# One chain of row statistics under transposes of the identity, own PSUM banks for the first projection, held spills, and earlier third gate weights

## The chip, the cores and the metric

The kernel runs on one core of one Trainium2 chip. The metric is the device time of one execution in microseconds (us). Three runs of the kernel before gave 2610.35, 2610.72 and 2611.09 us, so the median is 2610.72 us.

## What is computed

One block of attention with 32 heads, and beside it a gated feed-forward block on the same normalised rows. The silu of the feed-forward result gates the attention result.

```python
def _A_ref(x, wqkv, wo):                      # H = 32 heads of Dh = 18
    qkv = (x @ wqkv).reshape(B, S, 3, H, Dh).transpose(2, 0, 3, 1, 4)
    q, k, v = qkv[0], qkv[1], qkv[2]
    p = softmax(einsum("bhqd,bhkd->bhqk", q, k) * Dh ** -0.5)
    o = einsum("bhqk,bhkd->bhqd", p, v)
    return o.transpose(0, 2, 1, 3).reshape(B, S, D) @ wo

def _B_ref(x, W_gate, W_up, W_down):          # F = 4608
    gate, up = x @ W_gate, x @ W_up
    return (relu(gate) * up) @ W_down

xn = layernorm(x)                             # x: [1, 2048, 576] fp32
out = x + _A_ref(xn, wqkv, wo) * silu(_B_ref(xn, W_gate, W_up, W_down))
```

## The kernel before

All products are in fp32, made of pairs of fp32r numbers: each operand is split into a high part (a cast) and a low part (what the cast left over), and a product is the sum of hi x hi, hi x lo and lo x hi. So each weight and each activation costs a cast (on ScalarE or GpSimd) and a subtraction (on VectorE or GpSimd) before TensorE can use it. Weights are split on GpSimd by `split_pool` (lines 130 to 134).

The kernel has three stages. In the first (lines 302 to 644) the 2048 rows are taken in four groups g of 512. Of each group the rows are normalised, turned by TensorE into features x rows ("tps" banks), split, and kept as five tiles x of [128, 2, 512]. Then come the projections: four blocks b of q and k (`qk_block`, one `job` each, weights wqk0 to wqk3), the last 64 columns for two groups together (`qk_last`, wqk4), and four jobs of v (`v_job`, one for each 128 rows). A `job` (lines 469 to 479) issues 30 matmuls of its first part into two PSUM banks, then a tiny ScalarE instruction "mark" that waits for them, then the 24 matmuls of the second part of the job before (`flush`). The two halves of a job run side by side on the two halves of the array's rows. q, k and v go to DRAM (qd, kd, vd) by DMAs that GpSimd issues. `spill(g)` (lines 438 to 441) writes the five x tiles of a group to DRAM (xTd), four DMAs of 128 x 1024 fp32 (512 KB) and one of 64 x 1024. They are read back as nine tiles of 64 features by `load_x` (lines 293 to 300), two DMAs of 256 KB each, for the second stage.

The second stage takes the feed-forward block in 144 units (g, f): `up(k)` makes gate and up for 128 columns of F (27 matmuls on each half), `up_end` the product hh = relu(gate) x up and its split, and `down(k)`, after every second unit, adds two units' products into four y tiles. The gate and up weights of unit k are loaded by `load_up` into one of two buffers rg and split by `split_up` into one of two buffers gw. Between the matmuls of the units stand the attention matmuls: scores for the row maxima ("pm", 512 keys at a time), scores for the exponential ("psx") and the product with v ("po"). The row maxima of the first head pair begin already in the v jobs of the last group (`max_steps`, dealt one step per 18 matmul pairs). They read q and k of this pair from strips: q in the tile kq, the keys in four chunks c of 512 positions, chunk 0 in kA and chunks 1 to 3 in kq (`load_q`, `load_k`; six DMAs of 18 rows each). The third stage is the output projection.

What sets the order. The operations on TensorE, GpSimd and (up to unit 10) the DMAs issued by SyncE are kept in program order; each engine works its list from the front, and an instruction that waits holds up all behind it. SyncE issues all the loads, the spills and the strips; of the eight semaphores that its DMAs use in turn, each DMA waits until the one eight places ahead of it has landed. `load_x` in the second stage is not pinned after unit 10, so a scheduler may place it earlier.

Places that the change and the prediction speak of: `first_rows` (lines 387 to 420) normalises group 0, with two chains of statistics for rows 0, 1 and 2, 3 of its four row blocks, and splits wqk0 on ScalarE and VectorE; GpSimd's split of wqk1 waits for that (line 558). `next_pair` (line 445) hands out PSUM banks: "shared" is a pool of five, "bank" one of two, psO a single one. v weights are loaded in lines 564 to 568 and called at lines 603 to 607. `spill(g)` is called at line 638, the six loads `load_x(0, c)` behind it for g = 2 at line 641, `spill(3)` at line 575, and the gate weights of units 0 and 1 at lines 594 and 599. In `emit_unit` (line 863) the third weights, of unit 2, are loaded with unit 0 (line 869) and split with unit 1 (line 868).

## Time and profile before

| | us |
|---|---|
| median of three runs | 2610.72 |
| the profiled execution | 2611.43 |
| its span, first to last instruction | 2609.7 |
| granted TensorE clock, mean | 1.000 |
| VectorE busy | 1900.1 |
| ScalarE busy | 1383.3 |
| GpSimd busy | 1197.8 |

All times are of this one execution, in us from the start of its span. Rows of the timeline give start, duration, engine, source line, operation, tiles (out<-in), how many instructions are merged into the row, and in brackets the idle time of the engine before it with what ended it. PE is a matmul, PEld the weight load beside it, DVE is VectorE, ACT ScalarE, POOL GpSimd, SPq a DMA issued by SyncE. A row of the timeline whose engine is SPq shows the issuing alone; the data lands later. Rows of the windows give a stretch, its length, busy time and number of instructions for PE, PEld, DVE, ACT and POOL, the granted clock, the mean busy share of the 16 DMA engines, and GB/s.

### The profile page before, as it was taken

Reading aid. Unit: us, or ns where it says so; the run is one execution under the profiler, and the core shown is the slowest. Engines: PE = TensorE matmul, PEld = TensorE weight load, DVE = VectorE, ACT = ScalarE, POOL = GpSimd, SP = SyncE. Lnnn points to the kernel's source line nnn. Section 1 sums busy time; section 2 is a strip of 40 time slices with the busy share of each in tenths; the row PEclk is TensorE's granted clock in tenths of the full one; section 3 lists DMA queues with packets and bytes.
Section 4 is the critical chain, followed back from the end, with each engine's and each line's share of the span. In section 5 each row is a group of like instructions: output and inputs, shape, how many; then the busy total and the mean of one; then the engine's idle time right before and its main releaser. Section 6 shows DMA issues by size and latency. Waiting matters only on the chain.

```text
span 2609.7 us, 54494 instructions
## 1 busy us (share of the span) xinstructions
PE 2590.9 (99%) x21788; PEld 2035.6 (78%) x21788; DVE 1900.1 (73%) x3145; ACT 1383.3 (53%) x2594; POOL 1197.8 (46%) x971
## 2 busy tenths in 40 slices
PE   8999999999999999999999999999999999999999
PEld 7898887777777777777777777777777777777778
DVE  5335678788878788787887787887777878778235
ACT  2321135556665556555666555555556655555642
POOL 5246764344464434443455444444346444434554
PEclk9999999999999999999999999999999999999999
DMA  7867422222542322232363222222253232222245
GB/s 246 274 211 162 104 74 69 70 73 74 116 121 57 82 65 70 58 79 64 80 150 88 67 69 72 65 73 68 71 128 105 73 75 60 76 58 62 67 121 183
DMA packets 263806, 253.11 MB, mean 97 GB/s; under 512 B 27648, under 2 KB 208896, under 8 KB 263552
## 3 DMA queue, kind: packets, MB, share of 16 engines
q1 hardware_dynamic: 255808, 222.48, 32.9%
q0 software_dynamic: 7744, 27.14, 3.1%
q8 instruction: 172, 2.82, 0.5%
q14 instruction: 82, 0.67, 0.1%
HBM read 203.01 MB, written 46.01 MB: 95 GB/s over the span
## 4 chain that ended last, share of the span: by engine, by line
PE 97%; DMA 1%; POOL 1%; DVE 1%; issue 0%; ACT 0%; SPq 0%; POOLq 0%; DVEq 0%; ACTq 0%
PE pg L68 32%; PE po L68 19%; PE py L68 18%; PE pm L68 11%; PE psx L68 9%; PE pq L68 4%; PE pv L68 2%; PE pw L68 2%; DMA rg<-in_B_W_up_dram 0%; PE tps L76 0%; POOL wv L85 0%; DMA xt<-in_A_x_dram 0%; DMA ro<-od 0%; SPq L97 0%; DMA y<-gd 0%
## 5 line engine op out<-in xcount | busy, mean ns | idle before, releaser
L272 DVE TENSOR_REDUCE mx<-pm 128x1 f32<-128x512 f32 x2048 | 1363.9, 689 | 268.8 <-PE pm L68 148.9
L97 ACT ACTIVATE p<-psx 128x512 f32<-128x512 f32 x2048 | 1097.9, 603 | 583.0 <-PE psx L68 541.5
L68 PE MATMUL pg<-x,gw 64*128 64x512 f32 x7560 | 1372.8, 394 | 2.3 <-POOL gw L85 1.8
L68 PEld LDWEIGHTS pg<-x,gw 64*128 64x128 f32 x7560 | 1033.5, 186 | 85.9 <-issue 3.7
L85 POOL TENSOR_TENSOR hh<-h,hh 128x512 fp32r<-128x512 f32 x144 | 184.3, 1280 | 812.7 <-ACT hh L97 790.7
L68 PEld LDWEIGHTS py<-dw,hh 128*128 128x128 f32 x3456 | 460.1, 188 | 56.1 <-issue 31.8
L68 PE MATMUL py<-dw,hh 128*128 128x288 f32 x3456 | 476.8, 297 | 0.0
L68 PE MATMUL po<-p,va 128*32 128x512 f32 x4096 | 465.9, 595 | 0.0
L725 DVE TENSOR_TENSOR y<-py,y 128x288 f32<-128x288 f32 x544 | 244.3, 454 | 225.9 <-PE py L68 225.8
L85 POOL TENSOR_TENSOR gw<-rg,gw 128x1152 fp32r<-128x1152 f32 x144 | 385.9, 2680 | 11.6
L68 PEld LDWEIGHTS po<-p,va 128*32 128x32 f32 x4096 | 119.8, 109 | 276.2 <-issue 265.4
L85 POOL CAST dw<-rd 128x576 fp32r<-128x576 f32 x144 | 95.8, 665 | 387.7 <-PE py L68 382.1
L68 PE MATMUL psx<-qT,kq 56*128 56x512 f32 x608 | 229.8, 392 | 0.0
L68 PE MATMUL pm<-kq,qT 54*128 54x512 f32 x608 | 228.7, 398 | 0.1
L85 POOL TENSOR_TENSOR dw<-rd,dw 128x576 fp32r<-128x576 f32 x144 | 206.3, 1433 | 11.6
L97 ACT ACTIVATE hh<-h 128x512 fp32r<-128x512 f32 x144 | 90.8, 630 | 220.7 <-DVE h L696 220.7
L68 PE MATMUL psx<-kq,kA 56*128 56x512 f32 x512 | 195.4, 393 | 0.3 <-DVE h L696 0.2
L68 PE MATMUL pm<-kq 54*128 54x512 f32 x512 | 195.3, 402 | 0.0
L68 PE MATMUL psx<-kq 56*128 56x512 f32 x512 | 194.2, 392 | 0.0
L68 PE MATMUL pm<-kA,kq 54*128 54x512 f32 x512 | 193.6, 400 | 0.1
L85 POOL CAST gw<-rg 128x1152 fp32r<-128x1152 f32 x144 | 165.4, 1149 | 0.0
L68 PE MATMUL pm<-kA,qT 54*128 54x512 f32 x416 | 159.4, 402 | 0.0
(92 smaller groups left out, 2180.5 us busy)
## 6 DMA issues: line engine op xcount, KB each, us to landing
rg<-in_B_W_gate_dram SPq DMA_DIRECT2D x144, 288.0 KB
rg<-in_B_W_up_dram SPq DMA_DIRECT2D x144, 288.0 KB
rd<-in_B_W_down_dram SPq DMA_DIRECT2D x144, 288.0 KB
x<-xTd SPq DMA_DIRECT2D x72, 256.0 KB
qd<-hh POOLq DMA_DIRECT2D x16, 512.0 KB, 5.0
kd<-hh POOLq DMA_DIRECT2D x16, 512.0 KB, 6.1
xTd<-x SPq DMA_DIRECT2D x16, 512.0 KB
kq<-kd SPq DMA_DIRECT2D x210, 36.0 KB
```

Source lines behind the costliest of these rows:

```text
L68: return tc.keep_in_program_order(nc.tensor.matmul(*args, **kw))
L85: return lambda *args, **kw: tc.keep_in_program_order(op(*args, **kw))
L97: i = op(*args, **kw)
L272: vec(nc.vector.tensor_reduce(mx[:, h, b, j, c : c + 1], ps, axis=AX.X, op=ALU.max))
L725: vec(nc.vector.tensor_tensor(ys[j][:, cs], ps, ys[j][:, cs], ALU.add))
```

## The change

- `first_rows` makes one chain of statistics for all four row blocks. Before it TensorE transposes the identity 57 times into a bank that nothing reads. The cast of wqk0 stands behind the square root; its subtraction is cut in four, two pieces of 256 columns on VectorE and two of 384 and 256 on GpSimd, behind VectorE's.
- The first job takes its banks from the pool of two, not from the shared five.
- The v weights are loaded into three x tiles, early, and split one block earlier (`load_v`); the normalisation of group 1 is dealt every 9 steps and not every 7.
- `spill(g)` of groups 0, 1 and 2 gets a wait: its DMAs stay behind the mark of the group's second v job.
- The loads of x (`load_x`) are pinned to program order.
- The weights of unit 2 are loaded during the v jobs of the last group and split right behind the matmuls of unit 0, ahead of that unit's hh.
- Units 0, 2, ... 14 and 15 take psO and a shared bank, not units 1, 3, ... 15.

```diff
--- before.py
+++ after.py
@@ -127,10 +127,8 @@
         nc.scalar.activation(dhi, ps, AF.Copy)
         nc.vector.tensor_tensor(dlo, ps, dhi.bitcast(F32), ALU.subtract)
 
-    def split_pool(hi, lo, raw, behind=None):
-        cast = gp.tensor_copy(hi, raw)
-        if behind is not None:
-            after(cast, behind)
+    def split_pool(hi, lo, raw):
+        gp.tensor_copy(hi, raw)
         gp.tensor_tensor(lo, raw, hi.bitcast(F32), ALU.subtract)
 
     PRODUCTS = ((0, 0), (0, 1), (1, 0))
@@ -293,9 +291,11 @@
     def load_x(g, c):
         xc = xtile(xA)
         for t in range(2):
-            sp.dma_start(
-                xc[t * R : (t + 1) * R].rearrange("p a s -> p (a s)").bitcast(F32),
-                xTd[g, c // 2, c % 2 * R : c % 2 * R + R],
+            pinned(
+                nc.sync.dma_start(
+                    xc[t * R : (t + 1) * R].rearrange("p a s -> p (a s)").bitcast(F32),
+                    xTd[g, c // 2, c % 2 * R : c % 2 * R + R],
+                )
             )
         xcur.setdefault(g, []).append(xc)
 
@@ -305,7 +305,7 @@
         xB = pool(xBs, "xB", XC, "right")
         hx = pool(xBs, "hx", 4, "right")
 
-        def weights(name, n, parts, pl=one, held=None, behind=None, **kw):
+        def weights(name, n, parts, pl=one, held=None, **kw):
 
             sl = WS if len(parts[0]) == 2 else XC
             gw = homes_w[name] if name in homes_w else pl.tile([P, 2, WS, n], F32R, name=name, **kw)
@@ -318,12 +318,9 @@
                 hi, lo = gw[:, 0, :, o : o + m], gw[:, 1, :, o : o + m]
 
                 if held is not None:
-                    held += [
-                        lambda: pinned(nc.scalar.activation(hi, rg, AF.Copy)),
-                        lambda: vec(nc.vector.tensor_tensor(lo, rg, hi.bitcast(F32), ALU.subtract)),
-                    ]
+                    held += [hi, lo, rg]
                 else:
-                    split_pool(hi, lo, rg, behind)
+                    split_pool(hi, lo, rg)
                 o += m
             return gw
 
@@ -384,40 +381,34 @@
             split_full(xc[:, 0], xc[:, 1], ps)
             xs[g].append(xc)
 
-        def first_rows(xt, split_hi, split_lo):
+        def first_rows(xt, hi, lo, rg):
 
             xn = new_xn()
             banks = [shared("tps") for _ in range(XC)]
-            halves = [(0, 1), (2, 3)]
-            a, b = (stats(xt, js) for js in halves)
-
-            def finish(st_):
+            js = range(4)
+            steps = stats(xt, js)
+            while True:
                 try:
-                    while True:
-                        next(st_)
+                    next(steps)
                 except StopIteration as s:
-                    return s.value
-
-            def norm(js, ln):
-                for _ in normalize(xn, xt, js, *ln):
-                    pass
-
-            for _ in range(3):
-                next(a)
-            next(b)
-            ln = finish(a)
-            for _ in range(2):
-                next(b)
-            norm(halves[0], ln)
-            split_hi()
-            norm(halves[1], finish(b))
-            done = split_lo()
-            for j in range(4):
+                    ln = s.value
+                    break
+            pinned(nc.scalar.activation(hi, rg, AF.Copy))
+            for j, _ in enumerate(normalize(xn, xt, js, *ln)):
                 for c in range(XC):
                     turn(banks[c], xn, j, c)
+            rest = []
+            for s0 in (0, XC):
+                for on, ss in ((nc.vector, slice(s0, s0 + 2)), (None, slice(s0 + 2, min(s0 + XC, WS)))):
+                    args = lo[:, ss], rg[:, ss], hi[:, ss].bitcast(F32), ALU.subtract
+                    if on is None:
+                        rest.append(args)
+                    else:
+                        done = vec(on.tensor_tensor(*args))
+            for args in rest:
+                after(gp.tensor_tensor(*args), done)
             for ps in banks:
                 keep_x(0, ps)
-            return done
 
         def rows_to_features(g, xt):
 
@@ -435,15 +426,19 @@
                     keep_x(g, ps)
                 yield
 
-        def spill(g):
+        def spill(g, behind=None):
             for c in range(XC):
                 m = P if c < XC - 1 else R
-                sp.dma_start(xTd[g, c, :m], xs[g][c][:m].rearrange("p a s -> p (a s)").bitcast(F32))
+                out_ = sp.dma_start(xTd[g, c, :m], xs[g][c][:m].rearrange("p a s -> p (a s)").bitcast(F32))
+                if behind is not None:
+                    after(out_, behind)
 
         njob = [0]
 
         def next_pair(name):
             njob[0] += 1
+            if njob[0] == 1:
+                return [bank(name) for _ in range(2)]
             if njob[0] % 3:
                 return [shared(name) for _ in range(2)]
             return [shared(name), psO.tile([P, 512], F32, tag="po", name=name)]
@@ -466,6 +461,8 @@
                 run(*gens, P2)
                 done()
 
+        marks = []
+
         def job(outs, ops, done):
 
             fence = []
@@ -475,6 +472,7 @@
             for ins in fence:
                 after(seen, ins)
             fence.append(seen)
+            marks.append(seen)
             flush()
             pending.append((gens, done))
 
@@ -554,23 +552,35 @@
 
         held = []
         qk_weights(0, held=held)
-        w0_done = first_rows(rows0, *held)
-        qk_weights(1, behind=w0_done)
+        warm = bank("warm")
+        for _ in range(57):
+            tp(warm[:, :P], ident, ident)
+        first_rows(rows0, *held)
+        qk_weights(1)
         nxt = load_rows(1)
+        wvs = []
+
+        def load_v(m):
+            rg = xtile(xA).bitcast(F32).rearrange("p a s -> p (a s)")[:, : WS * VH]
+            rg = rg.rearrange("p (c f) -> p c f", f=VH)
+            load_nat(rg, [[(wqkv, 2 * D + o * HC + m * VH, VH)] for o in range(2)])
+            wvs.append(rg)
+
+        load_v(0)
         qk_weights(2)
         qk_weights(3)
+        load_v(1)
+        load_v(2)
         wv = one.tile([P, 2, WS, HC], F32R, name="wv")
 
         def v_weights(m):
-            rg = wr.tile([P, WS, P], F32, tag="rg", name="rgw")[:, :, :VH]
-            load_nat(rg, [[(wqkv, 2 * D + o * HC + m * VH, VH)] for o in range(2)])
             fs = slice(m * VH, (m + 1) * VH)
-            split_pool(wv[:, 0, :, fs], wv[:, 1, :, fs], rg)
+            split_pool(wv[:, 0, :, fs], wv[:, 1, :, fs], wvs[m])
 
         for g in range(NQ):
             last = g == NQ - 1
             fill = rows_to_features(g + 1, nxt) if not last else None
-            deal[:] = [fill, 7, 0]
+            deal[:] = [fill, 7 if g else 9, 0]
             if last:
                 spill(g)
             if g % 2:
@@ -600,10 +610,10 @@
                     split_up(0)
                 if b == 2 and last:
                     load_k(0, NQ - 1)
+                if b == 0 and g == 0:
+                    v_weights(0)
                 if b == 1 and g == 0:
-                    v_weights(0)
                     v_weights(1)
-                if b == 2 and g == 0:
                     v_weights(2)
                 if b == 1 and g == 1:
                     nxt = load_rows(g + 2)
@@ -625,6 +635,8 @@
                     v_job(wv, g, j, homes[j]())
                     if j == 0:
                         split_up(1)
+                    if j == 2:
+                        load_up(2)
                 deal[0] = None
                 flush()
                 for c in range(KC + 2 - XC, KC):
@@ -635,7 +647,7 @@
                     if j == 0 and g == 0:
                         nxt = load_rows(g + 2)
                     if j == 1:
-                        spill(g)
+                        spill(g, marks[-1])
                     if j and g == NQ - 2:
                         for c in range(2 * j - 2, 2 * j):
                             load_x(0, c)
@@ -664,7 +676,7 @@
 
         g, f = units[k]
         gw = gus.pop(k)
-        if k % 2 and k < N1:
+        if k < N1 and (k % 2 == 0 or k == N1 - 1):
             ps = [psO.tile([P, 512], F32, name="po"), shared("pg2")]
         else:
             ps = [bank("pg0"), bank("pg1")]
@@ -866,7 +878,8 @@
         if k not in rds and k not in dws:
             load_down(k)
         split_up(k + 1)
-        load_up(k + 2)
+        if k:
+            load_up(k + 2)
         if k == 10:
             sp.kept = False
         run_later()
@@ -895,6 +908,8 @@
             next(r)
             if i == 8:
                 gate_step()
+        if k == 0:
+            split_up(2)
         up_end(k, ps)
         while ready:
             attend()
```

TensorE, the first rows of the program. tps are the transposes of the normalised rows, pq the projections, wqk_109 the weights wqk0, and wqk_208 (before) and wqk_254 (now) the weights wqk1:

```order
-L76 MATMUL tps<-ident,xn 128x128 x20
-L68 MATMUL pq<-x,wqk_109 128x512 x30
-L68 MATMUL pq<-x,wqk_208 128x512 x30
```

```order
+L76 MATMUL warm<-ident 128x128 x57
+L76 MATMUL tps<-ident,xn 128x128 x20
+L68 MATMUL pq<-x,wqk_109 128x512 x30
+L68 MATMUL pq<-x,wqk_254 128x512 x30
```

The 57 transposes of the identity stand ahead of the twenty of the rows; the order of the jobs is as before.

SyncE's DMAs in group 2, from its spill (xTd<-x) on to the first loads of x for the second stage, with what each waits for (DMAHW0 to 7 are the eight semaphores of its own DMAs, Activation is ScalarE). Before:

```order
L97 DMA xTd<-x 128x1024 [waits DMAHW3_49,DVE_49]
L97 DMA xTd<-x 128x1024 [waits DMAHW4_49,DVE_49]
L97 DMA xTd<-x 128x1024 [waits DMAHW5_49,DVE_49]
L97 DMA xTd<-x 128x1024 [waits DMAHW6_49,DVE_49]
L97 DMA xTd<-x 64x1024 [waits DMAHW7_49,DVE_49]
L97 DMA x<-xTd 64x1024 [waits DMAHW0_49]
```

Now:

```order
L97 DMA xTd<-x 128x1024 [waits DMAHW3_49,DVE_49,Activation_49]
L97 DMA xTd<-x 128x1024 [waits DMAHW4_49,DVE_49]
L97 DMA xTd<-x 128x1024 [waits DMAHW5_49,DVE_49]
L97 DMA xTd<-x 128x1024 [waits DMAHW6_49,DVE_49]
L97 DMA xTd<-x 64x1024 [waits DMAHW7_49,DVE_49]
L295 DMA x<-xTd 64x1024 [waits DMAHW0_49,Pool_49]
```

The first DMA of the spill has a new wait on ScalarE, for the mark; the spills of groups 0 and 1 have the same. Behind these rows follow, before and now, in this order: eleven more loads of x, the five DMAs of the fourth group's spill, the gate and up weights of unit 0, six strips of q, six strips of kA (chunk 0), twelve of kq (chunks 1 and 2), the weights of unit 1, and six strips of kq (chunk 3). Now the weights of unit 2 stand behind these.

GpSimd around units 0 and 1. hh is a unit's product, dw a down weight, gw the gate and up weights; of gw, 2943 (before) and 2977 (now) belong to unit 2. Before:

```order
L85 MEMSET nm1_2844 128x32
L85 TENSOR_TENSOR hh_2935<-h_2933,hh_2935 128x512
L85 CAST dw_2938<-rd_2846 128x576
L85 TENSOR_TENSOR dw_2938<-rd_2846,dw_2938 128x576
L85 CAST gw_2943<-rg_2848 128x1152
L85 TENSOR_TENSOR gw_2943<-rg_2848,gw_2943 128x1152
L85 CAST dw_2949<-rd_2941 128x576
```

Now:

```order
L85 MEMSET nm1_2893 128x32
L85 CAST gw_2977<-rg_2748 128x1152
L85 TENSOR_TENSOR gw_2977<-rg_2748,gw_2977 128x1152
L85 TENSOR_TENSOR hh_2984<-h_2982,hh_2984 128x512
L85 CAST dw_2987<-rd_2895 128x576
L85 TENSOR_TENSOR dw_2987<-rd_2895,dw_2987 128x576
L85 CAST dw_2995<-rd_2990 128x576
```

The split of unit 2's weights moved ahead of unit 0's hh and the first down weight.

## The prediction

> **What bounds the kernel now.** First the page's span and its row of busy times, then the windows, to find where TensorE (PE) does not work.
>
> ```profile
> span 2609.7 us, 54494 instructions
> PE 2590.9 (99%) x21788; PEld 2035.6 (78%) x21788; DVE 1900.1 (73%) x3145; ACT 1383.3 (53%) x2594; POOL 1197.8 (46%) x971
> 0.00:20.00 20.00, 8.88 (x55) 7.53 (x57) 14.09 (x42) 6.41 (x14) 5.62 (x9) 1.00 0.72 215
> 40.00:100.00 60.00, 59.78 (x643) 52.08 (x642) 22.85 (x49) 17.90 (x46) 18.97 (x23) 1.00 0.91 317
> 140.00:160.00 20.00, 20.00 (x242) 19.10 (x240) 0.00 (x0) 3.92 (x14) 4.48 (x6) 1.00 0.42 124
> 200.00:220.00 20.00, 18.00 (x152) 16.76 (x154) 12.02 (x19) 2.77 (x6) 12.68 (x17) 1.00 1.07 230
> 500.00:2500.00 2000.00, 2000.00 (x16590) 1527.03 (x16588) 1547.98 (x2535) 1184.28 (x2179) 897.49 (x717) 1.00 0.31 79
> ```
>
> PE is busy in 2590.9 of 2609.7 us. Of the 18.8 us that are missing, 11.1 lie in the first 20 us and 2.0 between 200 and 220; from 500 to 2500 us nothing is missing. So only the opening and the passage from the first stage to the second have anything to give, and the change touches just these. What it can win there is small: 0.2% of the time, about what a measurement of this kernel can tell from no change, is 5.2 us. What it can lose is not bounded so: where PE's list meets a matmul whose data is late, everything behind it stands still. Hence two questions: how much of the small gaps goes, and does a moved transfer come too late for PE?
>
> **The opening.** Columns of a timeline row: start, duration, engine.
>
> ```profile
> 10.46 4.50 PE L76 MATMUL tps<-ident,xn 128*128 128x128 f32 x20 [10.46 <-DVE xn L368]
> 14.10 1.14 POOL L85 CAST wqk<-rgw 128x1152 fp32r<-128x1152 f32 x1 [12.79 <-DVE wqk L323]
> 14.14 2.56 ACT L127 ACTIVATE x<-tps 128x512 fp32r<-128x512 f32 x5 [1.08 <-PE tps L76]
> 14.77 3.08 DVE L128 TENSOR_TENSOR x<-tps,x 128x512 fp32r<-128x512 f32 x5 [0.74 <-ACT x L127]
> 15.33 2.68 POOL L85 TENSOR_TENSOR wqk<-rgw,wqk 128x1152 fp32r<-128x1152 f32 x1
> 15.52 18.43 PE L68 MATMUL pq<-x,wqk 64*128 64x512 f32 x154 [0.56 <-DVE x L128]
> 19.92 0.20 ACT L474 ACTIVATE mark<-ident 128x1 f32<-128x1 f32 x1 [3.22 <-PE pq L68]
> 33.88 1.10 PE L76 MATMUL tps<-ident,xn 128*128 128x128 f32 x8
> ```
>
> Before, twenty transposes took 4.50 us, 225 ns each, where later ones of the same form take 1.10/8 = 138 ns. So at 10.46 PE was slow from standing still, and fast by 15.52. The 57 transposes of the identity stand in the empty 10 us; at 225 ns they would take 12.8 us, at 138 ns 7.9. If PE turns fast on the way, the real ones gain 20 x 87 ns = 1.7 us, and the own banks let the first job start on ScalarE's first x tile, where it waited 0.56 us on VectorE. But the second job sets the end of it: it needs the low part of wqk1, done at 15.33 + 2.68 = 18.0. The change puts two pieces of wqk0 (384 + 256 of 1152 columns, 640/1152 x 2.68 = 1.5 us) before wqk1 on GpSimd and starts them about 1 us sooner than the cast's 14.10 of before (VectorE has half of its subtraction to do), so wqk1 is ready at about 18.6. The second job began behind the mark, at about 19.7. I take a gain of **1.1 us**; at most 2.6 (1.7 + 0.56, and some of the split), at least a loss of 0.5 if GpSimd starts no sooner.
>
> One rule speaks against this step. The Trainium skill says (TensorE: Matmul & The Clock Gate, Part 4: PE-mode transpose) that transposes do not count as work for the clock gate, so that PE stays slow through them. By that rule the 57 would heat nothing. This trace disagrees: nothing but the twenty transposes stood before 15.52, and the matmuls behind them ran at once at 18.43/154 = 120 ns.
>
> **Small waits that go.** The v weights are split earlier, which removes the first row below (0.2 us); unit 0 takes banks that no v job holds, which removes the 0.47 of the second. Together **0.7 us**, between 0 and 0.7.
>
> ```profile
> PE pv L68 <- POOL wv L85: 0.2, 1, 0.2
> 200.16 1.42 PE L68 MATMUL pg<-x,gw 64*128 64x512 f32 x9 [0.47 <-ACT ev L526]
>   PE pg L68: 1.8, 1
> 209.79 1.29 POOL L85 TENSOR_TENSOR hh<-h,hh 128x512 fp32r<-128x512 f32 x1 [5.33 <-ACT hh L97]
> 211.02 0.66 POOL L85 CAST dw<-rd 128x576 fp32r<-128x576 f32 x1
> 211.76 1.42 POOL L85 TENSOR_TENSOR dw<-rd,dw 128x576 fp32r<-128x576 f32 x1
> 213.13 1.14 POOL L85 CAST gw<-rg 128x1152 fp32r<-128x1152 f32 x1
> 214.35 2.62 POOL L85 TENSOR_TENSOR gw<-rg,gw 128x1152 fp32r<-128x1152 f32 x1
> 213.21 0.36 SPq L97 DMA_DIRECT2D rd<-in_B_W_down_dram  x1
> 218.00 0.67 POOL L85 CAST dw<-rd 128x576 fp32r<-128x576 f32 x1 [1.03 <-DMA rd<-in_B_W_down_dram]
> 223.71 6.54 PE py L68 x48
> ```
>
> **Third gate weights.** Unit 2 waited 1.8 us (third row; its weight load shows 2.3) until GpSimd had the low part of gw at 214.35 + 2.62 = 217.0. Now the split starts when unit 0's matmuls end. That is at about 207.7, since hh at 209.79 has three operations of some 0.6 us (relu, product, cast) between the last matmul and itself. With 1.14 + 2.62 us it is done at 211.5, before unit 2 asks for it at 217.0 - 2.3 = 214.7. That wait goes. What is late next: hh of unit 0 now ends at 212.8 and the first down weight (0.66 + 1.42 with gaps) at 214.9, 1.7 us later than before. The load of the second down weight waits for that buffer, so it is issued at 214.9 and not at 213.21. Before, it landed 4.8 us after its issue (218.00), behind the x loads that the old order had put there and the new one takes away. With the same 4.8 us its split ends at 221.8 and hh of unit 1 at 223.1, while `down(1)`, at 223.71 before, would come at 221.7: 1.4 us of wait at worst. I take a gain of **1.8 us**, between 0.5 and 2.0.
>
> Sum of the gains: 1.1 + 0.7 + 1.8 = **3.6 us**; by the ends of these ranges 0 to 5.3.
>
> **The held spills.** This is the part that I take to decide. The rows show SyncE's issues from 82.70 on, GpSimd's DMA traffic from 139 to 170 us (packets, MB, busy share), the mark, and the first score matmuls.
>
> ```profile
> 82.70 32.81 SPq L97 DMA_DIRECT2D x<-xTd  x12
> 124.66 6.16 SPq L97 DMA_DIRECT2D xTd<-x  x5
> 130.91 1.34 SPq L97 DMA_DIRECT2D rg<-in_B_W_gate_dram  x1
> 158.47 2.12 SPq L97 DMA_DIRECT2D kq<-qd  x6
> 165.72 2.53 SPq L97 DMA_DIRECT2D kA<-kd  x6
> 168.36 5.63 SPq L97 DMA_DIRECT2D kq<-kd  x12
> 174.04 0.60 SPq L97 DMA_DIRECT2D rg<-in_B_W_gate_dram  x1
> 175.43 3.45 SPq L97 DMA_DIRECT2D kq<-kd  x6
> q0 software_dynamic: 1203, 4.05, 43.9%
> 139.91 0.20 ACT L474 ACTIVATE mark<-ident 128x1 f32<-128x1 f32 x1 [0.97 <-PE pv L68]
> 179.54 0.46 PE L68 MATMUL pm<-kA,kq 54*128 54x512 f32 x2
> 184.97 0.85 PE L68 MATMUL pm<-kq 54*128 54x512 f32 x2
> 0.74 1.82 SPq L97 DMA_DIRECT2D xt<-in_A_x_dram  x4
> 3.60 0.82 DVE L347 BATCH_NORM_STATS2 stat<-xt 128x6 f32<-128x288 f32 x2 [3.60 <-DMA xt<-in_A_x_dram]
> ```
>
> Before, the spill of group 2 was out by 82.70, the twelve loads of x by 115.5, the fourth spill by 130.8, the first gate weights from 130.91; then SyncE idled until the q strips at 158.47. Now the spill of group 2 waits for the mark of that group's second v job, at 139.91 less the 1.3 us won so far, 138.6. In groups 0 and 1 nothing urgent stands behind the held spill. Here everything does: twelve loads, the fourth spill, the first gate weights, the q strips, the keys. SyncE works its list in order and runs at most eight DMAs ahead of what has landed.
>
> What must land before the last q strip, by the shapes of the tiles: two spills of 4 x 512 + 256 KB, twelve loads of 256, two weight loads of 288, six strips of 72, in all 8688 KB or 8.9 MB; and beside it GpSimd's 4.05 MB, since the two share the 16 engines. That is 12.95 MB. The stretch from 40 to 100 us, which held the same kinds of transfers and kept the engines 91% busy, moved 317 GB/s, or 348 at 100%. So 37 to 41 us. From 138.6 and 2.9 us for the first to land (issue at 0.74, used at 3.60) the last q strip lands at 179 to 182.5. The kA strips are a little behind, 182 to 185. PE asks for both at 179.54 - 1.3 = 178.2, so it stands 4 to 7 us in its first score matmul. Then chunks 1 and 2, unit 1's weights and chunk 3 are still to be issued: eighteen strips at about 0.45 us and two loads at 0.63, 9.4 us behind the first kA issue at about 181, and some 3 to 4 us to land: 194. PE reaches chunk 3 at 184.97 - 1.3 plus the 4 to 7 already lost, 188 to 191, and stands again for 3 to 6. I take a stall of **11 us** in all. Its ends: 3 us, if the engines go at 380 GB/s, so that q and chunk 0 are in time and only chunk 3 is late, and 17, if the two queues hinder each other more than in the stretch that I count by.
>
> A PE that stood may also run slow after it. Nothing in this trace shows a second slow phase; the opening bounds it, where twenty transposes lost 1.7 us: 0 to 1.7 for each of two stalls. I take **1.0**.
>
> The Trainium skill gives this a rule (TensorE: Matmul & The Clock Gate, Part 1): after one idle window of about 3.4 us the clock halves and stays so for about as long. By it the two stalls would cost about 3.4 us, an estimate from that page; here only the slow opening bears it out.
>
> Other edits cost nothing that I can find: pinned loads of x in later groups are issued behind unit 34's loads instead of long before, and needed a whole unit later, some 16 us (128 units in a little over 2000 us); the bank parity of the units leaves `down` between units 14 and 15, which hides the reuse of psO. If that cover failed, one ScalarE pass over a bank (2.56/5 = 0.5 us in the row at 14.14) would show once.
>
> **Sum.** -3.6 + 11 + 1.0 = +8.4 us on the profiled execution's 2611.43, so 2619.8. That execution stood 0.7 above the median 2610.72, so **2619.1**, and I write 2619.
>
> **Rivals.**
>
> (1) *The transfers keep up*, 0.17, the case on the other side. In the 20 us from 140 on the engines were only 42% busy, so there is room; decisive is whether 13 MB pass in under 37 us. If the last chunk lands by 184, no score matmul waits, and the time is 2610.7 - 3.6 = 2607 (up to 2610 with a small stall). For it: `x` loads and GpSimd's stores may overlap better than in the stretch counted. Against it: the one long stretch in which these transfers queued moved 317 GB/s.
>
> (2) *The warm-up does not warm, or lasts too long*, 0.08. The 57 stand in PE's list ahead of the real ones. At 225 ns each from about 1.4 us they end at 14.2, the real ones 4.5 later at 18.7, 3.7 later than the 14.96 of before; the wait for wqk1 hides there, so the opening loses about 2.8 instead of winning 1.1. With the stalls 2623, without them 2611. The skill's rule on transposes would give this; the 120 ns at 15.52 speak against it.
>
> (3) *The change does not do what it says*, 0.05: the hold has no weight because the mark comes early, or unit 2's wait comes back in `down(1)`. Then 2607 to 2612. The order above shows the wait, so I give it little.
>
> **Chances.** My forecast 0.70, the rivals 0.17, 0.08 and 0.05. Slower by over 0.2% (above 2616) needs a stall of more than 8 us or so: most of the 0.70 and most of rival 2, 0.69 in all. Faster by over 0.2% (below 2605.5) asks for every gain at its upper end and no stall: 0.03. Within 0.2%: 0.28. The range goes from rival 1's 2607 to the gains' half with a stall of 17 and two slow phases, 2610.7 - 1.5 + 17 + 3.4 = 2630.
>
> **What would show it.** The changed profile should have SyncE's x loads issued after 140 us and the q strips near 175 instead of 158.47; in 140 to 180 a DMA share near 0.9 and not 0.42 to 0.8; PE idle in front of pm, with a DMA kq or kA as releaser, near 178 and 188; no PE wait on gw before unit 2; unit 2's gw split near 208 plus the stall; the first pq near 14. If pm starts at about 178 with no wait, the held spills are harmless and I am wrong by the whole stall. If the waits are there but short, the rate of the DMA engines was my error.

## The result: 0.65% slower, and the profile after

The changed kernel takes 2627.28 us (median of five runs, 2624.76 to 2630.73) against 2610.72 us before in the same comparison (five runs, 2610.35 to 2611.23). The ratio is 1.0065, with a 95% interval from 1.0051 to 1.0078. The profiled execution took 2626.72 us, with a span of 2625.0.

First the waits of TensorE on data in the first 300 us of the changed kernel. Columns: who waits for whom, us in total, how often, the longest.

```profile
PE pm L68 <- DMA kq<-kd: 6.6, 2, 3.7
PE pm L68 <- DMA kA<-kd: 5.4, 1, 5.4
PE pv L68 <- POOL wv L85: 1.9, 2, 1.7
PE pg L68 <- DMA x<-xTd: 1.2, 1, 1.2
PE pq L68 <- POOL wqk L85: 0.4, 1, 0.4
```

The wait for gw before unit 2 is gone. In its place stand 12 us in front of the first score matmuls, 1.9 us for the v weights and 1.2 us for a chunk of x; of the last two the prediction had none. The timeline shows where they lie: the opening, the first v job, the release of the third spill (the second v mark of group 2), the issues behind it on SyncE's queue, the three stops at pm, and unit 0.

```profile
1.36 8.65 PE L76 MATMUL warm<-ident 128*128 128x128 f32 x57 [1.36 <-POOL ident masks.py:199]
10.20 2.40 PE L76 MATMUL tps<-ident,xn 128*128 128x128 f32 x20 [0.19 <-DVE xn L365]
18.00 12.34 PE L68 MATMUL pq<-x,wqk 64*128 64x512 f32 x106 [0.43 <-POOL wqk L85]
36.50 0.53 PE L68 MATMUL pv<-wv,x 64*128 64x288 f32 x4 [0.23 <-POOL wv L85]
38.73 0.40 PE L68 MATMUL pv<-wv,x 64*128 64x288 f32 x2 [1.70 <-POOL wv L85]
141.30 0.20 ACT L471 ACTIVATE mark<-ident 128x1 f32<-128x1 f32 x1 [0.97 <-PE pv L68]
146.40 13.41 SPq L295 DMA_DIRECT2D x<-xTd  x12
160.44 4.87 SPq L97 DMA_DIRECT2D xTd<-x  x5
169.33 11.55 SPq L97 DMA_DIRECT2D kq<-qd  x6
182.43 3.17 SPq L97 DMA_DIRECT2D kA<-kd  x6
186.61 1.37 PE L68 MATMUL pm<-kA,kq 54*128 54x512 f32 x2 [5.45 <-DMA kA<-kd]
195.71 0.47 PE L68 MATMUL pm<-kq 54*128 54x512 f32 x1 [2.86 <-DMA kq<-kd]
201.25 1.33 PE L68 MATMUL pm<-kq 54*128 54x512 f32 x2 [3.74 <-DMA kq<-kd]
225.63 0.50 PE L68 MATMUL pg<-x,gw 64*128 64x512 f32 x1 [1.21 <-DMA x<-xTd]
```

The twelve loads of x, which were issued from 82.70 on before, now come at 146.40. The q strips move from 158.47 to 169.33 and need 11.55 us to be issued instead of 2.12, because the queue ahead of them is full. The windows of the same execution have a second message. Columns: the stretch, its length, busy time of PE, PEld, DVE, ACT and POOL, the granted clock, the DMA share, GB/s.

```profile
36.65:40.06 3.41, 1.71 (x14) 1.18 (x14) 0.80 (x2) 1.54 (x5) 3.41 (x3) 1.00 0.09 36
40.06:43.47 3.41, 3.41 (x24) 3.11 (x24) 1.89 (x3) 0.99 (x3) 3.02 (x5) 0.50 0.99 357
140.00:160.00 20.00, 20.00 (x251) 19.16 (x249) 1.16 (x2) 4.20 (x14) 5.00 (x6) 1.00 0.93 299
160.00:180.00 20.00, 20.00 (x178) 19.77 (x176) 3.96 (x6) 3.98 (x9) 7.79 (x8) 1.00 1.01 345
180.00:183.42 3.42, 1.16 (x18) 0.92 (x14) 1.38 (x2) 1.20 (x2) 0.00 (x0) 1.00 0.44 147
183.42:190.25 6.83, 3.64 (x21) 3.22 (x23) 1.30 (x2) 0.20 (x1) 6.23 (x6) 0.50 0.44 130
190.25:197.07 6.82, 3.96 (x42) 3.28 (x39) 2.83 (x5) 1.19 (x2) 0.38 (x1) 1.00 0.99 316
197.07:207.31 10.24, 6.50 (x47) 5.90 (x46) 3.61 (x6) 0.20 (x1) 5.21 (x4) 0.50 0.97 233
```

From 140 to 180 us the DMA engines are full, at 299 and 345 GB/s. And the granted clock, which stood at 1.00 in all of the windows of before that the prediction shows, is 0.50 in three stretches: from 40.06 to 43.47 us behind the wait for the v weights, and from 183.42 to 190.25 and from 197.07 to 207.31 around the stops at pm.

Following one instruction through both executions gives the balance. The rows are starts of the tiny "mark" of a job on ScalarE and of the first matmul of `down(1)`:

| place | before | after | after later by |
|---|---|---|---|
| mark of the second job | 23.34 | 21.35 | -2.0 |
| mark of the second v job of group 0 | 48.93 | 50.34 | +1.4 |
| the same of group 2 (release of the third spill) | 139.91 | 141.30 | +1.4 |
| mark of the last v job | 196.15 | 214.66 | +18.5 |
| first py | 223.64 | 240.52 | +16.9 |
| end of the span | 2609.7 | 2625.0 | +15.3 |

So the opening wins 2.0 us (1.7, counted from the start of the first real transposes, which were 0.3 us earlier in this execution) and gives back 3.4 between 21 and 50 us: 1.9 of standing, and 3.41 us of work at half the clock, which costs 3.41 x 0.50 = 1.7 (together 3.6, so that the two account for all of it within 0.2). The passage past the third spill costs 17.1 us: 5.45 + 2.86 + 3.74 = 12.05 of standing, and 5.1 in which the array works at half the clock. PE is busy for 3.64 and 6.50 us of the two stretches at 0.50, and (3.64 + 6.50) x 0.50 = 5.07.

### The profile page after: what moved, and what is told of

Same layout as the page of the kernel before. It is cut to its first block, busy times and chain, and to the rows that moved or that the text cites. A ratio compares the mean times of both kernels' runs of the same rounds, so it can differ in the third digit from the quotient of the medians.

```text
span 2625.0 us, 54591 instructions
## 1 busy us (share of the span) xinstructions
PE 2602.8 (99%) x21845; PEld 2051.1 (78%) x21845; DVE 1898.5 (72%) x3140; ACT 1383.5 (53%) x2593; POOL 1199.7 (46%) x973
## 4 chain that ended last, share of the span: by engine, by line
PE 96%; DMA 2%; SPq 1%; POOL 1%; issue 0%; DVE 0%; ACT 0%; POOLq 0%; DVEq 0%
PE pg L68 32%; PE po L68 18%; PE py L68 18%; PE pm L68 11%; PE psx L68 9%; PE pq L68 3%; PE pv L68 2%; PE pw L68 2%; SPq L97 1%; DMA kq<-qd 1%; PE tps L76 0%; DMA x<-xTd 0%; DMA kq<-kd 0%; POOL wqk L85 0%; DMA xt<-in_A_x_dram 0%
```

## Experiments: which hold costs, and what the other edits are worth

Each ratio is against the kernel before, run on the same chip; "waits" are rows of the profiled execution.

**1. No hold at all.**

```diff
-                        spill(g, marks[-1])
+                        spill(g)
```

> The changed kernel, but no spill waits for a mark; all else stays. Theory (the hold pushes some 13 MB behind 141 us, and PE then stands 12.05 us at the first maxima and runs 4 us on a lower clock): the three waits at pm are gone, unit 0 begins at about 201 us and not 218, time 2608 to 2612 us. Rival (the strips are late because the third gate weights, the pinned loads of x and the v weights in x tiles changed the order of the queue): at least 5 us of waits at pm stay, 2616 us or more.

Measured: 2615.32 us (2611.01 to 2617.26), ratio 1.0014 (1.0005 to 1.0023). No wait at pm is left, so the hold made the strips late, as the theory has it, and the rival falls. But the time is 3 us above what I expected, because of a wait that the changed kernel did not have, and of 3.41 us at half the clock behind it (45.04 to 48.45). The rows are PE's waits, the timeline around 40 us and a window, in the kernel without holds:

```profile
PE tps L76 <- DVE x L128: 3.5, 1, 3.5
38.59 0.40 PE L68 MATMUL pv<-wv,x 64*128 64x288 f32 x2 [1.70 <-POOL wv L85]
39.94 1.47 PE L68 MATMUL pv<-wv,x 64*128 64x288 f32 x18
44.94 1.93 PE L76 MATMUL tps<-ident,xn 128*128 128x128 f32 x8 [3.53 <-DVE x L128]
29.27 3.58 SPq L97 DMA_DIRECT2D xTd<-x  x5
42.97 0.60 ACT L127 ACTIVATE hh<-pq 128x512 fp32r<-128x512 f32 x1 [2.96 <-DMA kd<-hh]
40.00:45.00 5.00, 1.47 (x20) 1.24 (x20) 2.09 (x4) 1.59 (x4) 1.14 (x2) 1.00 1.02 371
```

Read from the bottom: the DMA engines are full (share 1.02). ScalarE stands 2.96 us for a buffer hh that the store kd<-hh has not given back; that store shares the engines with the first spill, issued at 29.27. Behind this copy on ScalarE stands the one that frees a bank for PE's transposes. In the kernel before, the first spill was issued only at 43.75, since loads of weights that wait for their buffer rgw stood ahead of it:

```profile
27.96 15.05 SPq L97 DMA_DIRECT2D rgw<-in_A_wqkv_dram  x12
43.75 3.71 SPq L97 DMA_DIRECT2D xTd<-x  x5
```

The change loads the v weights into x tiles, ahead of this, and so it needs its hold on the first spill.

**2. Only the third spill held.**

```diff
-                        spill(g, marks[-1])
+                        spill(g, marks[-1] if g == 2 else None)
```

> The changed kernel with only the third spill held; the first two go as soon as their tiles are there. Theory (only the third hold stands ahead of the strips in SyncE's queue): waits of 11 to 13 us at pm as in the changed kernel, 2624 to 2629 us. Rival (the first two holds push their bytes on as well, so that all three add up): 4 us of waits or more are gone, 2622 us or less.

Measured: 2631.44 us (2630.21 to 2633.02), ratio 1.0075 (1.0061 to 1.0088). The waits at pm are 5.42 + 3.05 + 2.54 = 11.0 us, and the wait at the transposes is back with 3.9 us (3.5 in experiment 1). The time lies above the range that I gave, by the second wait, which the expectation does not count. The rival falls: taking the first two holds away does not shorten the stop.

**3. The kernel before, with the third spill held and nothing else.**

```diff
                     if j == 1:
-                        spill(g)
+                        spill(g, marks[-1] if g == 2 else None)
```

(`spill` takes the mark as in the change.)

> The kernel before with one thing added: the third spill held until the mark of its group's second v job. Theory: PE reaches the release at 139.9 us, the same bytes but for the 0.59 MB of the third gate weights come behind it, so 9 to 13 us of waits at pm and 3 to 5 us of a lower clock: 2622 to 2628 us. Rival (the hold hurts only beside the other edits): within 2 us of 2611.

Measured: 2628.66 us (2627.09 to 2632.65), ratio 1.0066 (1.0052 to 1.0080), just above the 2628 that I gave as the upper end. One wait, put into the kernel before, gives the whole loss of the change. PE's timeline in this run:

```profile
184.60 1.49 PE L68 MATMUL pm<-kA,kq 54*128 54x512 f32 x2 [4.95 <-DMA kA<-kd]
193.18 0.47 PE L68 MATMUL pm<-kq 54*128 54x512 f32 x1 [1.76 <-DMA kq<-kd]
199.69 1.44 PE L68 MATMUL pm<-kq 54*128 54x512 f32 x2 [4.84 <-DMA kq<-kd]
```

The stops are the same three, 11.6 us in all.

**4. Every hold released one v job earlier.**

```diff
-                        spill(g, marks[-1])
+                        spill(g, marks[-2])
```

> The changed kernel with each spill held until the mark of the group's first v job and not its second; for the third group that mark stands at 136.5 us and not 141.3. Theory (the queue is full from the release to the last strip): everything behind lands 4.8 us earlier, waits at pm 6 to 8.5 us and not 12.05, 2619 to 2623 us. Rival (a wait on a mark has a fixed price, whenever it is released): 2625 us or more. Rival (the strips wait for their source, not for the queue): waits unchanged.

Measured: 2624.30 us (2622.72 to 2624.63), ratio 1.0046 (1.0032 to 1.0060). The release of the third spill stands at 137.29 here and the mark after it at 142.05, so it is 4.8 us earlier. The stops answer to that:

```profile
183.63 0.94 PE L68 MATMUL pm<-kA,kq 54*128 54x512 f32 x2 [1.72 <-DMA kA<-kd]
189.38 0.47 PE L68 MATMUL pm<-kq 54*128 54x512 f32 x1 [0.18 <-DMA kq<-kd]
194.42 0.76 PE L68 MATMUL pm<-kq 54*128 54x512 f32 x1 [4.58 <-DMA kq<-kd]
197.99 1.38 PE L68 MATMUL pm<-kq 54*128 54x512 f32 x2 [0.65 <-DMA kq<-kd]
```

They sum to 7.13 us against 12.05: 4.8 us earlier takes 4.9 us of standing away, inside the 6 to 8.5 expected. Neither rival holds. The time fell by only 3 us, to above the range that I gave. From the release's job to the last v mark (142.05 to 211.45) the run takes 69.4 us, where before takes 56.24: 13.2 more, of which 7.1 is standing. Of the 6 that are left, 4.6 are work at half the clock: it stands at 0.50 from 194.01 to 204.25, and PE is busy for 9.18 us of that. The other 1.4 stay open. So less standing did not make the low clock much cheaper, 4.6 us here and 5.1 in the changed kernel.

**5. Only the first spill held, and 10. the first two.**

```diff
-                        spill(g, marks[-1])
+                        spill(g, marks[-1] if g == 0 else None)
```

> The changed kernel with only the first spill held; the second and third go as soon as their tiles are there. Theory (two holds of opposite worth: without the first, the first spill runs at 29 us beside the stores of q and k, PE then stands 3.5 us at 41 us for a bank that the split of hh frees; the third pushes the strips late): neither wait is there, 2608.5 to 2611.5 us, 3 to 5 us below the kernel with no hold. Rival (the 3.5 us come from something else than the first spill): 2613 to 2617 us, as without any hold.

Measured: 2610.79 us (2608.18 to 2613.34), ratio 0.9995 (0.9987 to 1.0004), 4.5 us below the kernel without holds. Neither the wait at pm nor the one behind DVE x is there. With the second spill held as well:

```diff
-                        spill(g, marks[-1])
+                        spill(g, marks[-1] if g < 2 else None)
```

> The changed kernel with the first and second spill held, not the third. Theory (only the third stands ahead of the strips, only the first beside the first stores of q and k; the second is without effect): as with the first alone, no wait at pm, 2609 to 2612 us. Rival (the second hold pushes bytes on to the third group): waits at pm or tps of over 1 us, 2613 us or more.

Measured: 2609.51 us (2607.39 to 2613.56), ratio 0.9994 (0.9985 to 1.0003). So one and the same line had three effects: the hold of group 0 saves some 4 us, that of group 1 does nothing that these runs can tell, that of group 2 costs 16 to 18 (experiment 2 against 1, experiment 3 against the kernel before, the changed kernel against experiment 10).

**6. The first hold, and the normalisation of group 1 dealt every 7 steps again.**

```diff
-            deal[:] = [fill, 7 if g else 9, 0]
+            deal[:] = [fill, 7, 0]
```

> As the kernel with only the first spill held, and the normalisation of group 1 dealt every 7 steps again and not every 9. Theory (with 9 the 20 transposes of group 1 stand behind the first matmuls of v, PE comes to the third split of the v weights 1.9 us too early and then runs on a lower clock to about 45 us): the transposes go first, PE reaches v at about 39 us, no wait for wv over 0.5 us, granted clock 1.00 from 40 to 100, at most 1.5 us of waits at tps: 2606 to 2609 us. Rival (the rows of group 1 are normalised so late that PE stands at the transposes instead): a wait of 2 us or more at tps, 2609 to 2612 us.

Measured: 2608.82 us (2606.87 to 2611.06), ratio 0.9990 (0.9981 to 0.9999). Where PE stood for wv in the changed kernel it now transposes first:

```profile
PE tps L76 <- DVE xn L365: 2.3, 3, 1.4
34.69 0.76 PE L76 MATMUL tps<-ident,xn 128*128 128x128 f32 x5 [0.74 <-DVE xn L365]
37.46 2.08 POOL L85 TENSOR_TENSOR wv<-x,wv 128x864 fp32r<-128x864 f32 x1
42.25 2.15 PE L68 MATMUL pv<-wv,x 64*128 64x288 f32 x30
```

The third split of the v weights ends at 39.5, and PE comes to v only at 42.25. Of the 2.3 us of waits for xn, 1.4 lie ahead of the first transposes (rows that came late in this execution), 0.9 at those of group 1; the clock stays at 1.00 from 40 on. PE reaches v later than the 39 us that I expected. The direction is as expected; the gain of 2 us over experiment 5 is not resolved, since the two intervals overlap.

**7. The same without the 57 transposes of the identity.**

```diff
-        warm = bank("warm")
-        for _ in range(57):
-            tp(warm[:, :P], ident, ident)
```

> As the kernel before it in this list, without the 57 transposes of the identity (nothing reads their bank). Theory (they warm the array): the 20 transposes of group 0 take 4.5 us again and not 2.4, the second job's mark comes 1 to 2 us later, time 0.5 to 2 us longer. Rival (the page's rule that transposes do not warm the array): the same 2.4 us or 4.5 us in both, mark and time within 0.5 us of the kernel with them. Other rival (the second job waits for GpSimd's split in any case): 4.5 us at the transposes, but the second mark unmoved.

Measured: 2609.78 us (2608.41 to 2613.20), ratio 0.9996 (0.9987 to 1.0005).

```profile
10.11 4.50 PE L76 MATMUL tps<-ident,xn 128*128 128x128 f32 x20 [10.11 <-DVE xn L365]
35.62 3.35 PE L68 MATMUL pq<-x,wqk 64*128 64x512 f32 x14
39.98 1.90 PE L68 MATMUL pq<-x,wqk 64*128 64x512 f32 x14
```

Without the 57 the real transposes take 4.50 us as in the kernel before, with them 2.40. And of the 57 themselves in the changed kernel the first 17 take 3.89 us, 229 ns each, while from 4.62 us on 42 take 5.39, 128 ns each. So transposes do warm the array here, against the rule of the Trainium skill that the prediction weighed (TensorE: Matmul & The Clock Gate, Part 4: PE-mode transpose). But the second mark comes at 22.15 us without them and at 22.48 with them (experiment 6, whose rows were ready 1.2 us later): the other rival is nearest, since the second job does not profit. Counted from the first real transpose the marks stand at 8.64 and 12.04 us without, 6.98 and 11.20 with them, so 1.7 us won at the first mark shrink to 0.8 at the second. The times are not apart.

**8. The kernel before, with the third gate weights early.**

```diff
+                    if j == 2:
+                        load_up(2)
...
-        load_up(k + 2)
+        if k:
+            load_up(k + 2)
...
+        if k == 0:
+            split_up(2)
         up_end(k, ps)
```

> The kernel before with one thing added: the weights of unit 2 are loaded during the v jobs of the last group and split behind the matmuls of unit 0. Theory: the wait of 1.84 us before unit 2 goes and no other takes its place: 2609 to 2610.5 us, 0.5 to 2.2 us below the kernel before. Rival (0.59 MB more ahead of the strips make the first maxima wait): a wait at pm of over 0.5 us, time the same or longer.

Measured: 2607.71 us (2606.97 to 2611.14), ratio 0.9989 (0.9980 to 0.9998): below both kernels, by 0.1% of the kernel before, and below the range that I gave. GpSimd and TensorE in this run:

```profile
206.72 1.15 POOL L85 CAST gw<-rg 128x1152 fp32r<-128x1152 f32 x1 [3.14 <-PE pm L68]
207.95 2.69 POOL L85 TENSOR_TENSOR gw<-rg,gw 128x1152 fp32r<-128x1152 f32 x1
220.37 6.62 PE L68 MATMUL py<-dw,hh 128*128 128x288 f32 x48
```

The split ends at 210.6, and no wait before unit 2 or before `down(1)` is left. From the last mark (195.27) to the first py PE takes 25.1 us, before 27.5: 2.4 us less. The span is 4.5 us shorter; the other 2.1 lie ahead of the last mark (0.9) and behind the first py (1.3), where the edit changes nothing that I can name.

**9. As experiment 6, with the units' banks of before.**

```diff
-        if k < N1 and (k % 2 == 0 or k == N1 - 1):
+        if k % 2 and k < N1:
```

> As the kernel with the first spill held and 7 steps, and the units' banks as in the kernel before (units 1, 3, ... 15 take psO and a shared bank). Theory (with a free second bank unit 0 begins both halves at once, and comes to its last chunk of x 1.5 us before that has landed): the wait of 1.5 us at pg for x goes, one of 0.5 us for the copy of v comes back before unit 0, 2607 to 2608.5 us. Rival (the load of x itself is late, whatever the banks): the wait for x stays over 1 us.

Measured: 2608.10 us (2606.34 to 2610.66), ratio 0.9989 (0.9980 to 0.9997). The wait for x is gone and the one of 0.47 us for the copy of v is back:

```profile
199.80 1.42 PE L68 MATMUL pg<-x,gw 64*128 64x512 f32 x9 [0.47 <-ACT ev L524]
```

With the new banks unit 0 begins 3.4 us after the last mark (experiment 6), both halves at once (pg and po alternate from its first row on), and PE asks for the last chunk of x before it has landed; with the old banks it begins 4.0 us after the last mark. That this later start is the whole reason is not shown, for the wait in experiment 6 was 1.55 us. The first py stands at 221.16 here and at 222.69 in experiment 6, of which 0.7 was there at the last mark already. In time the two do not differ.

**11. The kernel before, with the early weights of unit 2 and the opening of the change** (one chain, 57 transposes, banks of the first job, pinned loads of x; v weights, spills, 7 steps and units' banks as before):

```diff
+        warm = bank("warm")
+        for _ in range(57):
+            tp(warm[:, :P], ident, ident)
...
-        w0_done = first_rows(rows0, *held)
-        qk_weights(1, behind=w0_done)
+        first_rows(rows0, *held)
+        qk_weights(1)
```

> The kernel before with the early weights of unit 2, the opening of the change (one chain, 57 transposes, banks of the first job) and pinned loads of x; v weights, spills, 7 steps and the units' banks are as before. Theory (the opening brings PE 1 to 1.7 us forward at the second mark, but PE then comes to the third split of the v weights that much earlier, and that split is bound by GpSimd at about 41 us): a wait of 1 to 2.5 us for wv, 2606.5 to 2609 us, within 1 us of the kernel before with early weights alone. Rival (the gain of the opening reaches the end): no wait for wv over 0.6 us, 2605 to 2606.5 us.

Measured: 2609.16 us (2608.63 to 2610.62), ratio 0.9992 (0.9983 to 1.0001). The wait for wv is there, as the theory expected. The time lies just above the 2609 that I gave as the upper end, and 1.5 us above experiment 8, where I had expected it within 1:

```profile
40.71 2.04 POOL L85 TENSOR_TENSOR wv<-rgw,wv 128x864 fp32r<-128x864 f32 x1
42.80 1.99 PE L68 MATMUL pv<-wv,x 64*128 64x288 f32 x26 [1.36 <-POOL wv L85]
```

PE is ready for v 1.36 us before GpSimd has split it. What the opening wins, the next wait takes.

## Why the prediction was right, step by step

The sign, the place and the main mechanism were right; the time of 2627 lies inside the range and 8 us above the forecast of 2619. By the spans of the two profiled executions the change is +15.3 us where the sum says +8.4, so 6.9 more. PE's slow work makes 4.1 of that, the opening with the v weights 2.7 (1.3 to be won, 1.4 lost), unit 0's banks 1.2 and the held spills 1.1. Against these, the third gate weights won 0.6 more than I took, and 1.6 fell away behind the first py.

- **The held spills, 11 us: right.** Measured 12.05. Release, full queue, late q strips, and stops at chunk 0 (5.45 us, forecast 4 to 7) and at chunk 3 (3.74, forecast 3 to 6) came as described. The stop of 2.86 us between them, at the second head's keys of chunk 2, I had not named. Experiments 3, 4 and 10 show the cause: the third hold alone gives the loss, without it the loss is gone, and its stops move with the moment of release, one for one. The rate was right too: 299 and 345 GB/s in the two windows, 322 on average, where I counted with 317 to 348. Only the release came at 141.3 instead of 138.6, because the opening's gain had been lost by then; PE came to its first stop later by as much (181.2 and not 178.2), so that this error left the stop as it was.
- **PE slow after standing, 1.0 us: mis-sized, it measured 5.1.** I bounded it by the one slow phase of the old trace, 1.7 for each of two stalls, and took less than half of that. The changed kernel has two slow stretches, and both are long: 6.83 and 10.24 us at 0.50, of which PE worked 3.64 and 6.50, so they cost 1.8 and 3.3 us. Behind the second of the three stops the clock was still at 1.00. The rule of the Trainium skill that stood beside that term (TensorE: Matmul & The Clock Gate, Part 1: half the clock, for about 3.4 us) gives by estimate 3.4 us for two stalls and 5.1 for three. That the latter equals what was measured is luck: this trace does not have three phases of 3.4 us but two, of two and three times that length.
- **The opening, 1.1 us: inside its range at the second mark, wrong at the end.** 2.0 us were won there, where I had allowed 2.6 at most; the wait for wqk1 (0.43 us, to 18.00) is the bound that I named, though GpSimd was done 0.6 us sooner than the 18.6 I took. The step that failed came after it: I counted the earlier v weights as a gain of 0.2 us and did not ask what PE meets when it comes earlier. With 9 steps the 20 transposes of group 1 stood behind the start of v, PE came to the splits of the v weights 1.9 us too soon, and the clock fell: 3.4 us lost in place of 0.2 won. Experiment 6, with the 7 steps of before, has neither the stop nor the slow clock (experiment 5, with 9 steps, has the stop alone), and experiment 11 shows a wait for the same split under the old place of the v weights.
- **Unit 0's banks, 0.5 us: the wait went, a dearer one came.** 0.47 us gone, 1.21 us for the last chunk of x in its place; experiment 9 turns this round.
- **Third gate weights, 1.8 us: right.** The wait went without another in its place; the 1.4 us in `down(1)` that I held possible did not come (experiment 8).
- **"Pinned loads and other edits cost nothing": not contradicted.** After the first py the spans of before and after differ by 1.6 us, 2386.1 against 2384.5 us. Experiments 8 and 9 take 2384.8 and 2384.6, with the loads of x unpinned in 8 and pinned in 9, so pinning does not explain it. I leave it open.
- **That the holds of groups 0 and 1 are harmless** I had argued from what stands behind them on SyncE's queue. For group 1 that is so. For group 0 it was half of the answer: experiments 1 and 5 show that this hold earns some 4 us beside the early v loads; that it does so by keeping the spill out of the way of the stores of q and k is read from the rows of experiment 1.

Of the rivals, the first (transfers keep up) is refuted by the stops, the second (the warm-up does not warm) by the 2.40 us, the third by the vanished wait before unit 2.

The two fastest versions are experiments 8 and 9, both with a ratio of 0.9989 and intervals below 1. The early weights of unit 2 are the only part whose gain shows by itself; with the first hold, 7 steps and the old banks the rest of the change costs nothing, and has no gain that these runs can tell.

## What to carry to other kernels

A wait on a queue that is worked in order delays all that stands behind it. Before adding one, list for every iteration what follows in the queue and when it is needed; here the same line helped in the first group, did nothing in the second and cost 16 us or more in the third. When a step makes the bottleneck engine arrive earlier, name the next operand that it meets, with the time at which that is ready, or the gain turns into a stop. And price a stop of TensorE by more than its length: each one may be followed by slow work.

## What the runs showed of the hardware that was not expected

Short stops lowered the clock, and not every time. Read in windows of 0.2 us over the first 260 us, the granted clock is 1.00 or 0.50, with values between only where a window holds the change, and every stretch at 0.50 in these runs lasts 3.4, 6.8 or 10.2 us. Within one execution the stretches start whole multiples of 3.41 us apart: 42.0 and 4.0 times in the changed kernel (40.06, 183.42, 197.07), 44.0 and 4.0 in experiment 2 (40.42, 190.60, 204.26), 4.0 in experiment 3 (182.45, 196.10), 45.0 in experiment 4 (40.41, 194.01). So in these traces the clock changes only at the ends of a window of 3.41 us that runs on through the whole execution.

This tells why equal stops had unequal effects. The stop for the third split of the v weights is 1.70 us long in the changed kernel and in experiment 1. In the first it lies whole in one window (36.65 to 40.06 in the rows of the result: PE busy 1.71 of 3.41 us), and the next window has a clock of 0.50. In experiment 1 the end of a window cuts it, and the clock stays:

```profile
34.80:38.21 3.41, 2.03 (x18) 1.21 (x14) 1.81 (x2) 0.61 (x3) 3.33 (x3) 1.00 1.03 421
38.21:41.62 3.41, 2.82 (x28) 2.28 (x28) 0.69 (x1) 0.60 (x1) 2.25 (x4) 1.00 1.03 401
```

Counted by such windows in the seven runs that have a stretch at 0.50 (the changed kernel, experiments 1 to 5 and 7), a window at full clock in which PE stood for up to 1.4 us was never followed by half the clock, and one with 1.74 us or more always was. Between these it went both ways: 1.47 (experiment 7, two stops of 0.73 and 0.75 us), 1.59 (experiment 5) and 1.70 us lowered the clock, 1.56 (experiment 2) and 1.72 (experiment 4) did not, and what decides there stays open. The clock came back only behind a window in which PE did not stand at all. At half the clock eighteen v matmuls took 2.53 us and not 1.46 to 1.47. The Trainium skill describes such a window (TensorE: Matmul & The Clock Gate, Part 1: The HAM clock gate): about 3.4 us, running freely, with half the clock after at least one idle window. The length and the free run agree with these traces; but here a window that was idle for half its length was enough.

The granted clock does not show every slow phase. It stands at 1.00 in the first 20 us of the kernel before, though the twenty transposes there took 225 ns each; that phase is read from the durations alone.

From one execution to the next the opening moves by about a microsecond, whatever the kernel: group 0's first transposes began between 9.72 (experiment 8) and 11.28 us (experiment 6). Differences below that cannot be read off the starts of rows of a single execution.
